# Sparse attention followed by an ELU feed-forward layer: load order, load shapes and the hand-written engine orders rewritten

## The chip, the cores and the metric

The kernel runs on one core of a Trainium2 chip. The metric is device time in microseconds (us), the median of the runs of one build. The core has a matrix engine (TensorE, PE in the profile; its weight loads are PEld), VectorE (DVE), ScalarE (ACT), GpSimd (POOL), SyncE (SP, which here only starts stores and transposing transfers), and 16 DMA engines that move data between memory (HBM) and the on-chip SBUF. PSUM is the accumulator memory; it is used here as two "pairs" of two banks (slots 0 and 1) and four single banks (slots 2 to 5).

## The reference

Inputs are q, k, v of shape (8 batches, 8 heads, 576 positions, 64) in float32. Heads 0 to 3 of each batch use a *local* causal mask (a key counts if it lies 0 to 31 positions back), heads 4 to 7 a *strided* causal mask (a key counts if it lies a multiple of 32 positions back). The attention output is a matrix of 4608 tokens by 512, and it passes through a two-layer network:

```
scores = q @ k.T / 8;  scores = where(mask, scores, -1e9)
attn   = softmax(scores);  x = attn @ v            # x: 4608 tokens x 512
h = x @ w_in                                       # w_in: 512 x 2048
g = where(h > 0, h, exp(min(h, 0)) - 1)            # ELU
out = g @ w_out                                    # w_out: 2048 x 512
```

## The kernel before

All matrix work is in bfloat16; GpSimd's transfers convert from float32 on the way. The work is named by short tokens in one long list, `ORDER` (lines 48 to 147), which the loop at line 797 issues one after the other. Each engine executes its own instructions strictly in that order, so the list decides what each engine queues behind what. A token names its work, `@n` the PSUM slot and `/D`, `/A` or `/S` the engine that copies (DVE, ACT, or a transposing transfer from SP).

Attention tokens begin with batch, kind (`l` local, `s` strided) and head pair (0 or 1). For the first three batches q and k are turned on PE: `tq`, `tk` (lines 434 to 448) transpose into PSUM and `cq`, `ck` (450 to 462) copy back to SBUF. Batches 3 to 7 use `turn`, transposing transfers. `S`, or for batch 0 `s0` and `s1`, computes scores; `e`, `F0`, `F1` (or `e0`, `e1`) are exponentials on ACT; `m0` and `M` multiply by a 0/1 mask on DVE. Where a batch and kind stand in `ADDED` (line 230), the mask is instead added to the scores by extra matmuls with an identity matrix, and no `m` is needed. `v0`, `v1` copy the strided v into place, `halo` copies the last 32 rows of each block of local v in front of the next block (line 496), `a` is probabilities times v, `n` the division by the row sum (a reciprocal and a product on DVE, lines 647 and 649), `x` transposes the result on PE and `y` copies it into `xT`, the input of the network.

The network runs in nine chunks of 512 tokens. In chunk c, `i c.b` (line 725) computes hidden block b of 16 as four matmuls of 128x128 by 512 columns (a third number names one of the four, in the order strided pair 0, strided pair 1, local pair 0, local pair 1); `x` is the exponential (ACT, line 730), `r` the clipping on DVE (line 736) or a ReLU on ACT (line 734), `g` the last step of ELU on DVE (lines 745, 742). `o c.t.p` (line 751) computes quarter p (hidden blocks 4p to 4p+3) of the output of 128 tokens, and `c` copies the finished output to SBUF for its store. `busy.n` are n matmuls on zeros, of no use to the result.

Chunk 0 needs only batch 0; chunk c above 0 needs batches up to c. The loads of the first batches, the masks, the clearing of buffers and the weights are issued by GpSimd in the order of `LOADS` (line 41): `l.q.0` is the local q of batch 0, `s.v.1` the strided v of batch 1, `w.in.2` the third of four quarters of w_in (hidden blocks 8 to 11), `w.out.2` the third quarter of w_out. The strided q and k of batch 0 are issued ahead of the list (line 384). The part of the list from `clear.v.2` on is issued where `load.2` stands in `ORDER`. Later batches are loaded by the tokens `load.3` to `load.7`.

In the kernel before, the strided attention of batch 1 is computed among that of batch 0, ahead of the first matmul of the network, and the rest of batch 1 within chunk 0. The strided v of a batch is loaded by one transfer per head of 90 partitions and one of 18 partitions for what is left (lines 262 to 269); the local v by one transfer (line 274); w_out by four transfers whose partitions take one row of 2 KB from each of four blocks of 128 rows (line 327).

Of the kernel before, what the change touches and what calls it, by code (L numbers as in the profile page):

```python
# [41 lines left out]
l.q.0 s.v.0 l.k.0 s.q.1 mask.cut.0 s.k.1 l.v.0 s.v.1 w.in.0 l.k.1 w.in.1 w.in.2 l.q.1  # L42
w.out.0 w.in.3 clear.str.0 clear.loc.1 clear.loc.2 w.out.1 clear.str.1 w.out.2
clear.loc.0 l.v.1 mask.late.0 w.out.3 clear.v.2 s.q.2 s.k.2 s.v.2 l.q.2 l.k.2 l.v.2
# [4 lines left out]
0s1.tq@2 0s0.tq@3 0s1.cq/D 0s0.cq/D busy.3 0s1.tk@4 0s0.tk@2 0s1.ck/D 0s0.ck/D  # L49
0s0.s0@0 0l0.tq@3 0s0.e0 0l1.tq@4 0l0.cq/A 0s1.s1@1 0l1.cq/D 0s1.s0@0 0s1.e1 0s0.v0/D  # L50
0s0.v1/A 0s0.s1@1 0s1.e0 mk.s 0s0.e1 busy.2 0s1.a@0 0l0.tk@2 0s1.n@0 0l1.tk@3 0l0.ck/A
0s0.a@1 0l1.ck/A 0l0.s0@0 0s0.n@1 load.2 0s1.x@4 1s0.tq@2 0l0.e0 1s1.tq@3 0s1.y/D
0l1.s0@1 1s1.cq/A 0l1.s1@0 1s0.cq/D 0l1.e0 0s0.x@4 1s0.tk@3 0l1.e1 0l0.s1@1 0s0.y/D
1s0.ck/A 1s1.tk@2 0l0.e1 mk.l 1s1.ck/A busy.3 1s0.S@0,1,4,3 0s1.halo/D 1s0.e 1s0.v0/D
1s0.F0 busy.3 0l0.a@0 1s0.v1/D 1s1.e 1s0.m0 0l0.n@0 1s0.F1 busy.1 0l1.a@1 0l1.n@1
busy.2 0l0.x@2 i0.1.0@4 i0.2.0@5 0l0.y/A i0.1.1 i0.0.0@3 1s0.M 0l1.x@0 1s1.m0 i0.0.1
i0.1.2 0l1.y/D i0.0.2 1s0.a@1 i0.0.3 i0.1.3 1s0.n@0 1l0.tk@2 x0.0@0 i0.2.1 x0.1@1
i0.2.2 i0.2.3 r0.0/D 1s0.x@0 r0.1/D 1l1.tk@1 x0.2@2 g0.0 r0.2/D i0.6@3 1l1.ck/D g0.2
1s1.a@1 x0.6@0 g0.1 i0.4@5 1s1.n@1 i0.5@4 x0.4@2 r0.6/D 1s1.x@1 1s0.y/D r0.4/A x0.5@1
g0.4 1s1.y/A 1l1.tq@0 r0.5/D i0.3@5 1l1.cq/A g0.6 g0.5 1l0.tq@1 x0.3@2 i0.7@3 1l0.ck/D  # L60
# [48 lines left out]
o4.1.0@3 5s0.F1 5s1.e 5s0.M c4.0/D o4.1.1 5s1.m0 5s0.a@0 o4.1.2 5s0.n@0 5s1.a@1 o4.1.3
5s1.n@1 5s0.z o4.2.0@4 c4.1/A 6l0.S@0,1,5,2 5s1.z o4.2.1 6l0.e o4.2.2 6l0.F0 6l0.m0  # L110
6l0.F1 6l1.e o4.2.3 6l0.M o4.3.0@3 6l1.m0 c4.2/A o4.3.1 turn.7l o4.3.2 o4.3.3 5s0.y/A
c4.3/D 6s0.v0/D 6s0.S@0,1,5,2 5s1.y/A 6s0.v1/D i5.0@4 6s0.e turn.7s i5.1@3 6s0.F0
6s0.m0 x5.0@1 i5.2@5 6s0.F1 r5.0/D x5.1@2 6s0.M 6s1.e g5.0 i5.3@2 r5.1/D x5.2@0
6s0.a@0 6s1.m0 x5.3@1 g5.1 i5.4@4 r5.2/A r5.3/D x5.4@2 g5.2 i5.5@3 g5.3 r5.4/A i5.6@5
x5.5@0 g5.4 i5.7@2 r5.5/A 6s0.n@0 x5.6@1 o5.0.0@4 x5.7@2 g5.5 6s0.z r5.6/A r5.7/D
i5.8@3 g5.6 6s1.halo/A g5.7 6s1.a@1 i5.9@5 x5.8@0 6s1.n@1 r5.8/A 6l0.a@0 x5.9@1
i5.10@2 g5.8 6s1.z r5.9/A 6l0.n@0 6l1.a@1 x5.10@2 i5.11@3 g5.9 r5.10/A o5.0.1 6l0.y/S
x5.11@0 6l1.n@1 i5.12@5 r5.11/A g5.10 6l1.y/S g5.11 x5.12@1 i5.13@2 r5.12/D i5.14@3
g5.12 6s0.y/A o5.0.2 x5.13@2 x5.14@0 r5.13/D i5.15@5 g5.13 r5.14/A g5.14 o5.1.0@2
x5.15@1 r5.15/D 6s1.y/A o5.1.1 g5.15 o5.1.2 7l0.S@0,1,3,5 o5.0.3 7l0.F1 7l0.F0 7l0.e  # L120
o5.1.3 7l0.M c5.0/D 7l1.e i6.0@5 7l0.m0 c5.1/D i6.1@3 x6.0@2 7l1.m0 i6.2@4 r6.0/D
x6.1@0 g6.0 i6.3@2 r6.1/A x6.2@1 g6.1 i6.4@5 x6.3@2 r6.2/D o5.2.0@3 g6.2 r6.3/A x6.4@0
g6.3 i6.5@4 r6.4/D i6.6@2 g6.4 x6.5@1 7s0.v0/D i6.7@5 r6.5/D x6.6@2 g6.5 o5.2.1 x6.7@0
r6.6/D 7s0.v1/D i6.8@4 g6.6 r6.7/A g6.7 i6.9@2 x6.8@1 i6.10@5 r6.8/D x6.9@2 g6.8
o5.2.2 r6.9/A x6.10@0 g6.9 i6.11@4 r6.10/D o5.2.3 g6.10 x6.11@1 7s0.S@0,1,2,5 r6.11/D
c5.2/A g6.11 i6.12@3 7s0.F1 7s0.F0 7s0.e 7s0.M o5.3.0@4 7s1.e 7s0.m0 i6.13@5
7s1.halo/D x6.12@2 7s0.a@0 7s1.m0 x6.13@0 7l0.a@1 7s0.n@0 o5.3.1 r6.12/A r6.13/A
# [23 lines left out]
def kernel(  # L151
# [75 lines left out]

    E_STR, E_LOC = 3, 3

    ADDED = ('0l', '0s')  # L230
    src = {"q": q, "k": k, "v": v}


# [150 lines left out]
    for name in "qk":  # L384
        load_strided(0, name)
# [603 lines left out]
```

## Time and profile before

| | |
|---|---|
| median of 3 runs | 315.29 us (315.17 to 315.65) |
| the profiled execution | 314.54 us, of which the traced span is 312.7 us |
| PE, PEld busy | 297.9 us (95%), 147.8 us (47%) |
| DVE, ACT busy | 217.5 us (70%), 189.5 us (61%) |
| POOL busy | 136.0 us (43%) |
| granted PE clock | 0.996 of full speed |
| first matmul of the network | 25.16 us after the span's start |

The span runs from the first to the last instruction. An engine's busy time counts each moment once; the "mean ns" of a PE row is the time from issue to the modelled end of one matmul, and since matmuls follow each other in a pipeline, the distance between their starts is what a matmul costs. The chain of work that ended last gives these distances. Its shares: PE 82%, DVE 5%, POOL 4%, DMA 3%.

### The profile page before, as it was taken

What the parts mean: (1) busy time and instruction counts of PE and PEld (TensorE: products, weight loads), DVE (VectorE), ACT (ScalarE), POOL (GpSimd) and SP (SyncE); (2) the same over time, 40 slices, a digit from 0 to 9 for tenths busy, and PEclk for the clock granted to TensorE, in tenths of its full rate; (3) what the DMA queues carried; (4) which work ended last, traced back from release to release, by engine and by line L of the source; (5) the groups of instructions that cost most, each with busy time, mean ns of one, the idle gap of its engine ahead of it and who ended that gap; (6) DMA issues with size and microseconds to landing.
All of it is one profiled execution on the core that took longest, in us unless ns stands there. A gap on an engine that the chain in (4) does not pass through costs nothing.

```text
span 312.7 us, 6031 instructions
## 1 busy us (share of the span) xinstructions
PE 297.9 (95%) x2222; PEld 147.8 (47%) x2262; DVE 217.5 (70%) x424; ACT 189.5 (61%) x346; POOL 136.0 (43%) x207
## 2 busy tenths in 40 slices
PE   8888899999999999999999999999999999999992
PEld 3554446445545544445444454544454444444441
DVE  2578987687969886797288865996888178765300
ACT  4683685686847766565476648986675167555210
POOL 8959954698777776984894500000000000000000
PEclk9999999999999999999999999999999999999998
DMA  6999999999999999999999966731005311012012
GB/s 102 176 160 206 207 170 153 166 82 136 165 152 191 162 155 106 147 223 161 204 150 168 157 127 111 148 61 67 0 36 114 72 31 34 8 39 60 34 69 74
DMA packets 116357, 37.37 MB, mean 119 GB/s; under 512 B 97320, under 2 KB 111280, under 8 KB 116320
## 3 DMA queue, kind: packets, MB, share of 16 engines
q0 software_dynamic: 74240, 18.42, 66.4%
q1 hardware_dynamic: 42080, 18.49, 31.6%
q8 instruction: 19, 0.31, 0.4%
q14 instruction: 18, 0.15, 0.2%
HBM read 36.70 MB, written 9.44 MB: 148 GB/s over the span
## 4 chain that ended last, share of the span: by engine, by line
PE 82%; DVE 5%; POOL 4%; DMA 3%; issue 2%; ACT 2%; POOLq 0%; ACTq 0%
PE single L751 39%; PE single L725 37%; DMA w_in_sb<-in_moe_w_in_dram 3%; PE pair L637 3%; DVE g_sb L745 2%; DVE g_sb L736 2%; POOL v_raw L263 2%; PE pair L544 1%; ACT e_sb L730 1%; PE single L544 1%; PE pair L446 1%; DVE x_s L649 1%; PE pair L657 1%; POOL v_loc L274 0%; POOL v_raw L267 0%
## 5 line engine op out<-in xcount | busy, mean ns | idle before, releaser
L725 PE MATMUL single<-xT,w_in_sb 128*128 128x512 bf16 x555 | 135.7, 379 | 2.9 <-DVE g_sb L745 1.1
L751 PE MATMUL single<-w_out_sb,g_sb 128*128 128x512 bf16 x560 | 134.6, 379 | 1.4 <-issue 0.3
L730 ACT ACTIVATE e_sb<-single 128x512 f32<-128x512 f32 x144 | 85.4, 599 | 71.2 <-PE single L725 67.6
L725 PEld LDWEIGHTS <-w_in_sb 128*128 128x128 bf16 x576 | 54.6, 98 | 65.0 <-issue 2.4
L751 PEld LDWEIGHTS <-g_sb 128*128 128x128 bf16 x576 | 54.4, 98 | 62.5 <-issue 0.5
L745 DVE TENSOR_TENSOR g_sb<-g_sb,single 128x512 bf16<-128x512 bf16 x92 | 62.4, 684 | 2.1
L736 DVE TENSOR_SCALAR g_sb<-e_sb 128x512 bf16<-128x512 f32 x92 | 44.0, 480 | 28.5 <-ACT e_sb L730 27.8
L742 DVE SCALAR_TENSOR_TENSOR g_sb<-e_sb,g_sb 128x512 bf16<-128x512 f32 x52 | 35.5, 686 | 7.5 <-ACT g_sb L734 7.5
L622 ACT ACTIVATE pr<-pair 128x960 bf16<-128x960 f32 (+4 forms) x36 | 31.7, 900 | 6.0 <-PE pair L544 3.2
L734 ACT ACTIVATE g_sb<-single 128x512 bf16<-128x512 f32 x52 | 30.7, 593 | 0.0
L758 ACT COPY o_sb<-single 128x512 f32<-128x512 f32 x23 | 13.5, 587 | 22.6 <-PE single L751 21.8
L263 POOL DMA_DIRECT2D v_raw<-in_v_dram x32 | 20.0, 640 | 3.8 <-DMA v_loc<-in_v_dram 2.2
L637 PEld LDWEIGHTS <-pr 128*128 128x128 bf16 (+3 forms) x364 | 15.3, 102 | 8.6 <-issue 3.1
L758 DVE COPY o_sb<-single 128x512 f32<-128x512 f32 x12 | 8.2, 687 | 13.7 <-PE single L751 13.7
L286 POOL DMA_DIRECT2D k_loc<-in_k_dram x20 | 15.1, 773 | 5.3 <-DMA v_loc<-in_v_dram 2.3
L286 POOL DMA_DIRECT2D q_loc<-in_q_dram x20 | 15.4, 780 | 2.8 <-DMA k_str<-in_k_dram 2.6
L649 DVE TENSOR_TENSOR x_l<-pair,rden 96x768 bf16<-96x768 f32 x16 | 15.3, 954 | 0.6
L649 DVE TENSOR_TENSOR x_s<-pair,rden 126x640 bf16<-126x640 f32 (+1 forms) x16 | 14.0, 874 | 0.5
L626 DVE TENSOR_TENSOR pr<-pr,mask_l 128x960 bf16<-128x960 bf16 x14 | 9.2, 654 | 6.1 <-ACT pr L622 6.1
L263 POOL DMA_DIRECT2D q_str<-in_q_dram x20 | 12.8, 646 | 0.1
L263 POOL DMA_DIRECT2D k_str<-in_k_dram x20 | 12.4, 631 | 1.2 <-DMA q_str<-in_q_dram 0.6
L274 POOL DMA_DIRECT2D v_loc<-in_v_dram x8 | 9.8, 1220 | 2.7 <-issue 1.6
(121 smaller groups left out, 232.7 us busy)
## 6 DMA issues: line engine op xcount, KB each, us to landing
out_dram<-o_sb SPq DMA_DIRECT2D x30, 256.0 KB, 2.8
v_loc<-in_v_dram POOLq DMA_DIRECT2D x8, 288.0 KB, 9.0
v_raw<-in_v_dram POOLq DMA_DIRECT2D x32, 67.5 KB, 6.1
w_in_sb<-in_moe_w_in_dram POOLq DMA_DIRECT2D x4, 512.0 KB, 10.3
w_out_sb<-in_moe_w_out_dram POOLq DMA_DIRECT2D x4, 512.0 KB, 11.6
out_dram<-o_sb SPq DMA_DIRECT2D x12, 128.0 KB, 2.3
q_str<-in_q_dram POOLq DMA_DIRECT2D x20, 67.5 KB, 6.7
k_str<-in_k_dram POOLq DMA_DIRECT2D x20, 67.5 KB, 5.4
```

The source lines that it names most:

```text
L263: nc.gpsimd.dma_start(out=t[0:n, h, 0:run].rearrange("p g d -> p (g d)"), in_=rows[h, :, 0:30, :].rearrange("t (a g) d -> a t (g d)", g=run))
L286: nc.gpsimd.dma_start(out=t[:, h // 2, 0:4, h % 2], in_=src[name][b, h, 0:512].rearrange("(i p) d -> p i d", p=128))
L622: nc.scalar.activation(t, sc[0:t.shape[0], :, 0:w], ACT.Exp, scale=scale)
L637: nc.tensor.matmul(av[0:m, p, blk, :], lhsT=self.pr[0:k, o:o + m], rhs=vt[0:k, 2 * self.hp + p, blk, :], start=True, stop=True)
L649: nc.vector.tensor_tensor(self.x[0:nq, 0:n].rearrange("q g p d -> q p g d"), av[0:nq, :, 0:n, 0:D], rd[0:nq, :, 0:n].unsqueeze(3).to_broad ...
L725: nc.tensor.matmul(h_of[c, i], lhsT=w_in_sb[:, cc, i * 128:(i + 1) * 128], rhs=xT[:, cc, c * N_TILE:(c + 1) * N_TILE], start=j == 0, stop= ...
L730: nc.scalar.activation(e_sb[slot], h_of[c, i], ACT.Exp)
L734: nc.scalar.activation(g[:, i, :], h_of[c, i], ACT.Relu)
L736: nc.vector.tensor_scalar(g[:, i, :], e, scalar1=1.0, scalar2=1.0, op0=ALU.min, op1=ALU.subtract)
L742: nc.vector.scalar_tensor_tensor(g[:, i, :], e, 1.0, g[:, i, :], op0=ALU.subtract, op1=ALU.min)
L745: nc.vector.tensor_tensor(g[:, i, :], g[:, i, :], h_of[c, i], op=ALU.max)
L751: nc.tensor.matmul(out_of[c, i], lhsT=g[:, m, i * 128:(i + 1) * 128], rhs=w_out_sb[:, m, :], start=(m == 0), stop=(m == MC - 1))
```

## The change

`LOADS` has a new order: the weights come ahead of all of batch 1, and the local q and k of batch 0 come ahead of its v. The local q of batch 0 is issued before the identity matrix and the masks are built. The strided v of the first three batches is loaded in six transfers of 18 partitions, each over all four heads; the local v of batch 0 in two transfers, one per pair of heads, and its halo copy is made per pair. w_out is loaded with four consecutive rows on one partition, and so hidden unit p*4+j takes the place that unit j*128+p had; the columns of w_in are therefore read with a step of four when they are loaded as matmul weights (`w_in_part`). Batch 1's local scores get their mask by added matmuls. The mask of the first local block is that of the others. `ORDER` is written anew throughout; the part shown ends where chunk 1 begins.

```diff
 LOADS = """
-l.q.0 s.v.0 l.k.0 s.q.1 mask.cut.0 s.k.1 l.v.0 s.v.1 w.in.0 l.k.1 w.in.1 w.in.2 l.q.1
-w.out.0 w.in.3 clear.str.0 clear.loc.1 clear.loc.2 w.out.1 clear.str.1 w.out.2
-clear.loc.0 l.v.1 mask.late.0 w.out.3 clear.v.2 s.q.2 s.k.2 s.v.2 l.q.2 l.k.2 l.v.2
+l.q.0 l.k.0 s.v.0 mask.cut.0 l.v.0 w.in.0 w.in.1 w.out.0 w.in.2 clear.loc.2 w.in.3
+w.out.1 w.out.2 clear.loc.1 clear.str.1 clear.str.0 l.q.1 l.k.1 s.q.1 mask.late.0
+clear.loc.0 w.out.3 s.k.1 l.v.1 s.v.1 clear.v.2 l.q.2 l.k.2 s.q.2 s.k.2 s.v.2 l.v.2
 ORDER = """
+0s0.tq@2 0s1.tq@3 0s0.cq/D 0s1.cq/D busy.3 0s1.tk@4 0s0.tk@2 0s1.ck/D 0s0.ck/D
+0s0.s0@0 0l0.tq@3 0s0.e0 0s0.s1@1 0l0.cq/A 0l1.tq@4 0s0.e1 0s1.s0@0 0l1.cq/D 0l1.tk@2
+0s1.e0 0l0.tk@3 0l1.ck/A 0s1.s1@1 0l0.ck/D 0l1.s0@0 0s1.e1 0s0.v1/D 0s0.v0/D 0l1.e0
+mk.s busy.1 0l0.s1@1 load.2 0l1.s1@0 0l0.e1 0l1.e1 busy.1 0s0.a@1 0s1.a@0 0s0.n@0
+0l0.halo/A 0s1.n@1 busy.2 0l0.s0@1 0s0.x@4 0l0.e0 busy.1 0s1.x@2 0s0.y/D 0l1.halo/A
+0l0.a@0 mk.l 0s1.y/A 0l1.a@1 0l0.n@0 0l1.n@1 busy.2 0l0.x@3 i0.0.0@4 0l0.y/A i0.1.0@2
+0l1.x@0 i0.2.0@3 i0.0.1 0l1.y/D i0.0.2 i0.0.3 i0.1.1 i0.2.1 x0.0@0 i0.2.2 i0.1.2
+i0.1.3 r0.0/D i0.2.3 i0.3@5 g0.0 x0.1@1 x0.2@2 r0.1/D i0.4@4 g0.1 r0.2/A x0.3@0 g0.2
...
+i0.14@3 g0.12 o0.0.1 r0.15/D
+x0.14@0 g0.15 1l0.tq@5 r0.14/A 1l1.tq@2 g0.14 1l0.cq/A o0.0.2 1l1.cq/A 1l0.tk@5
+1l1.tk@3 1l0.ck/A o0.1.0@2 1l1.ck/A 1s0.tq@5 1s1.tq@3 o0.1.1 1s0.cq/D 1s1.cq/D
+1l0.S@0,1,5,3 o0.0.3 1l0.e o0.1.2 1l0.F0 c0.0/D 1l0.F1 1l1.e 1s0.tk@5 1s1.tk@3 o0.1.3
+1s0.ck/D 1s1.ck/D 1s0.S@0,1,4,5 c0.1/A o0.2.0@3 1s0.e 1s1.halo/D o0.2.1 1s0.F0 1s0.m0
+1s0.F1 1s1.e 1l0.a@0 1s0.M o0.2.2 1s0.v0/D 1s0.v1/D 1s1.m0 1s0.a@1 1l0.n@0 o0.2.3
+o0.3.0@2 1s0.n@0 c0.2/A 1s1.a@0 1s0.x@4 1s1.n@1 1l0.x@5 1l1.a@1 1s0.y/A 2l0.tq@3
+1l0.y/D 1s1.x@4 2l0.cq/A 2l1.tq@0 1l1.n@1 o0.3.1 1s1.y/A 2l1.cq/D 1l1.x@5 2l0.tk@3
+1l1.y/D load.3 2l1.tk@4 2l0.ck/A i1.0@5 2l1.ck/A i1.1@3 x1.0@1 2s0.tq@4 r1.0/D
...
+def w_in_part(w_in_sb, c, i):
+    return w_in_sb[i // 4][:, c].rearrange("k (p j) -> k j p", j=4)[:, i % 4]
-    w_in_sb = consts.tile([128, KC, d_ff], BF16, tag="w_in_sb")
+    w_in_sb = several(consts, 4, "w_in", KC, 512)
-    ADDED = ('0l', '0s')
+    ADDED = ('0l', '0s', '1l')
...
+        if b < E_STR:
+            for a in range(6):
+                r = slice(run * a, min(run * a + run, STRIDE))
+                nc.gpsimd.dma_start(
+                    out=t[NT * a:NT * a + NT, :, 0:r.stop - r.start, :].rearrange(
+                        "p h g d -> p h (g d)"),
+                    in_=rows[:, :, r, :].rearrange("h t g d -> t h (g d)"))
+            return
...
-            nc.gpsimd.dma_start(
-                out=v_loc[b % 3].rearrange("p h i d -> p (h i) d")[32:128, :, 0:D],
-                in_=v[b, 0:4].rearrange("h (i p) d -> p (h i) d", p=LB))
+            for h in (slice(0, 2), slice(2, 4)) if b == 0 else (slice(0, 4),):
+                nc.gpsimd.dma_start(
+                    out=v_loc[b % 3][:, h].rearrange("p h i d -> p (h i) d")[32:128, :, 0:D],
+                    in_=v[b, h].rearrange("h (i p) d -> p (h i) d", p=LB))
...
-            nc.gpsimd.dma_start(out=w_in_sb[:, :, 512 * i:512 * (i + 1)],
+            nc.gpsimd.dma_start(out=w_in_sb[i],
                                 in_=wi[:, :, 512 * i:512 * (i + 1)])
-            nc.gpsimd.dma_start(out=w_out_sb[:, 4 * i:4 * (i + 1), :],
-                                in_=wo[:, 4 * i:4 * (i + 1), :])
+            nc.gpsimd.dma_start(
+                out=w_out_sb[:, 4 * i:4 * (i + 1), :].rearrange("p j d -> p (j d)"),
+                in_=moe_w_out[512 * i:512 * (i + 1)].rearrange("(p j) d -> p (j d)", j=4))
...
     for name in "qk":
         load_strided(0, name)
+    load(LOADS[0])
...
         def halo(self, copy, slot):
             t = v_loc[self.b % 3]
+            if self.b == 0:
+                t = t[:, 2 * self.hp:2 * self.hp + 2]
             copy(t[0:32, :, 1:6, 0:D], t[96:128, :, 0:5, 0:D])
...
-                nc.tensor.matmul(h_of[c, i], lhsT=w_in_sb[:, cc, i * 128:(i + 1) * 128],
+                nc.tensor.matmul(h_of[c, i], lhsT=w_in_part(w_in_sb, cc, i),
```

Counted over the whole list, 82 of the 144 `r` steps are on DVE and 62 on ACT (before 92 and 52), and of the first 35 `c` copies 4 are on DVE and 31 on ACT (before 12 and 23; the last is shared by both in either kernel). The `busy` matmuls in the list are 10 (before 14).

197 lines of the change are left out of this document (89 added, 108 removed).

## The prediction

> **What bounds the kernel now.** I read the page first, then the busy time by stretches, then the chain and single rows of the time order around the first network matmul. The page:
>
> ```profile
> span 312.7 us, 6031 instructions
> ...
> L725 PE MATMUL single<-xT,w_in_sb 128*128 128x512 bf16 x555 | 135.7, 379 | 2.9 <-DVE g_sb L745 1.1
> ...
> L730 ACT ACTIVATE e_sb<-single 128x512 f32<-128x512 f32 x144 | 85.4, 599 | 71.2 <-PE single L725 67.6
> L725 PEld LDWEIGHTS <-w_in_sb 128*128 128x128 bf16 x576 | 54.6, 98 | 65.0 <-issue 2.4
> ...
> L745 DVE TENSOR_TENSOR g_sb<-g_sb,single 128x512 bf16<-128x512 bf16 x92 | 62.4, 684 | 2.1
> L736 DVE TENSOR_SCALAR g_sb<-e_sb 128x512 bf16<-128x512 f32 x92 | 44.0, 480 | 28.5 <-ACT e_sb L730 27.8
> ...
> L734 ACT ACTIVATE g_sb<-single 128x512 bf16<-128x512 f32 x52 | 30.7, 593 | 0.0
> L758 ACT COPY o_sb<-single 128x512 f32<-128x512 f32 x23 | 13.5, 587 | 22.6 <-PE single L751 21.8
> ```
>
> The reader sees that ACT waited 67.6 us for PE, and PE little for anything: PE sets the pace. The stretches tell where it does not (columns: stretch, length, busy us of PE, PEld, DVE, ACT, POOL; at the end clock, DMA share and GB/s):
>
> ```profile
> 10.00:20.00 10.00, 9.11 (x179) 6.21 (x180) 6.01 (x16) 8.46 (x15) 6.05 (x9) 1.00 1.76 161
> 20.00:30.00 10.00, 8.39 (x121) 4.92 (x121) 7.48 (x18) 5.22 (x10) 9.86 (x13) 1.00 1.26 204
> 30.00:40.00 10.00, 8.15 (x69) 4.13 (x71) 9.93 (x19) 6.11 (x12) 9.65 (x15) 1.00 1.25 206
> 40.00:60.00 20.00, 19.84 (x179) 10.48 (x180) 14.02 (x28) 13.21 (x25) 12.04 (x17) 1.00 1.61 165
> 60.00:80.00 20.00, 19.36 (x188) 9.89 (x190) 16.86 (x33) 16.00 (x31) 16.89 (x25) 1.00 1.28 114
> 80.00:300.00 220.00, 217.53 (x1406) 105.20 (x1433) 159.45 (x304) 134.99 (x242) 72.87 (x108) 1.00 0.90 109
> ```
>
> From 40 us on PE idles little: 0.64 us from 60 to 80, 2.47 us from 80 to 300. Ahead of 40 us it idles, and part of its busy time is matmuls on zeros. In 30 to 40 us DVE is busy 9.93 of 10: there batch 1's attention and chunk 0 share it. So the ends to work on are the first network matmul, and DVE right behind it. What released that matmul stands in the order of time and in the chain:
>
> ```profile
> 10.22 0.65 ACT L622 ACTIVATE pr<-pair 108x576 bf16<-108x576 f32 x1 [0.27 <-PE pair L544]
> ```
> ```profile
> 24.30 0.95 DVE L649 TENSOR_TENSOR x_l<-pair,rden 96x768 bf16<-96x768 f32 x1
> ```
> ```profile
> 25.16 1.04 PE L725 MATMUL single<-xT,w_in_sb 128*128 128x512 bf16 x4 [0.54 <-DMA w_in_sb<-in_moe_w_in_dram]
> ```
> ```profile
> 14.93 10.19 DMA w_in_sb<-in_moe_w_in_dram
> ...
> 36.94 0.38 PE pair L446 x12
> ...
> 43.47 2.59 PE single L725 x12
> ...
> 47.94 0.21 PE pair L544 x10
> ...
> 51.96 0.76 PE pair L637 x24
> 52.72 0.52 PE single L440 x16
> ...
> 54.11 0.26 PE single L657 x6
> ```
>
> Two things end together at 25.2 us: the first weights land (14.93 + 10.19 = 25.12) and the last division of batch 0 (24.30 + 0.95 = 25.25). Taking away one alone gives nothing. The chain also prices PE work by start distance: a network matmul is 2.59 / 12 = 0.216, a block or output quarter of four 0.864.
>
> **Term 1, the loads.**
>
> ```profile
> w_in_sb<-in_moe_w_in_dram POOLq DMA_DIRECT2D x4, 512.0 KB, 10.3
> w_out_sb<-in_moe_w_out_dram POOLq DMA_DIRECT2D x4, 512.0 KB, 11.6
> ...
> k_loc<-in_k_dram POOLq DMA_DIRECT2D x3, 288.0 KB, 7.7
> ```
> ```profile
> w_out_sb<-in_moe_w_out_dram POOLq DMA_DIRECT2D x1, 512.0 KB, 10.7
> ```
> ```profile
> 38.48 0.77 POOL L327 DMA_DIRECT2D w_out_sb<-in_moe_w_out_dram  x1
> ```
> ```profile
> POOL w_in_sb L324 <- DMA v_loc<-in_v_dram: 2.5, 1, 2.5
> ```
>
> A load of q, k or v is 288 KB, a quarter of weights 512 KB. Ahead of the first quarter stood nine 288 KB loads; the change leaves six. Three of them are 885 kB; at the 161 to 206 GB/s of the stretches that is 4.3 to 5.5 us, so w.in.0 lands near 20.2. At 205 GB/s a quarter takes 2.56 us and a 288 KB load 1.44: w.in.1 22.8, w.out.0 25.3, w.in.2 27.9, w.in.3 30.5, then w.out.1, w.out.2, l.q.1 37, l.k.1 38.5, s.q.1 40, w.out.3 42.5, s.k.1 44, and s.v.1 near 49, as the last load of the same set did before (38.48 + 10.7). In the program each GpSimd transfer waits for the eighth before it; a 2.5 us wait of that kind is the row above. In the new order what stands in the queue behind each such wait is masks, memsets and further loads, and several 512 KB quarters are always under way, so I cost these waits, the sixth v slice and the split local v at nothing; without that cover a late load costs PE its lateness (first rival).
>
> **Term 2, batch 0's attention.**
>
> ```profile
> L649 DVE TENSOR_TENSOR x_l<-pair,rden 96x768 bf16<-96x768 f32 x16 | 15.3, 954 | 0.6
> ...
> L649 DVE TENSOR_TENSOR x_s<-pair,rden 108x768 bf16<-108x768 f32 x6 | 5.7, 958 | 0.2
> L647 DVE RECIPROCAL rden<-pair 96x12 f32<-96x12 f32 x16 | 3.6, 222 | 1.1 <-PE pair L637 1.1
> ...
> L461 DVE COPY kT_loc<-pair 128x576 bf16<-128x576 bf16 x2 | 1.5, 738 | 0.0
> L686 DVE COPY xT<-single 128x540 bf16<-128x540 bf16 x2 | 1.4, 721 | 0.8 <-PE single L657 0.8
> ...
> L454 DVE COPY kT_str<-single 128x576 bf16<-128x576 bf16 x3 | 1.3, 450 | 0.3 <-PE single L440 0.3
> ```
> ```profile
> L622 ACT ACTIVATE pr<-pair 108x972 bf16<-108x972 f32 x4 | 3.9, 969 | 0.6 <-PE single L544 0.6
> ...
> L461 ACT COPY qT_loc<-pair 128x576 bf16<-128x576 bf16 x4 | 2.6, 640 | 0.1
> ...
> L622 ACT ACTIVATE pr<-pair 128x576 bf16<-128x576 f32 x4 | 2.5, 655 | 0.5 <-PE pair L544 0.5
> ```
>
> The first exponential stays at 10.22: what it needs is not moved. ACT then does seven exponentials of 0.65 and two copies of 0.64, 5.8 us, and with two short waits for PE ends near 16.5. The first division follows at 16.6, and DVE is then the chain: two strided divisions (0.96 plus two reciprocals, 1.2), one copy into xT (0.72 and its small rest, 0.9), the mask (0.3), two local divisions (1.18): 6.0, so 22.6 instead of 25.25. The v loads land by 13 (strided) and 17 (local) and are due at 15.5 and 17 to 19. Batch 0's halo copies now stand on ACT and wait there for the halves of local v; behind them queue the last local exponential, due at 18.5, and the copies into xT, so a half that lands after 18.5 delays the divisions by as much. Weights, at 20.2, no longer decide. The first complete block has all four inputs at 23.7.
>
> **Term 3, chunk 0 and batch 1.** From there DVE spends per block 0.684 and, in about half of them, 0.48: 0.92, against PE's 0.864. PE needs for 16 blocks and two output quarters 15.6 us from 21.9, plus about 1.2 of waits for DVE at start: 38.7. Then 12 quarters (10.4), and attention: local transposes of batches 1 and 2, 8 x 0.38; strided ones of batch 1, 2 x 0.52; scores of 1 1.3; four `a` 1.5, four `x` 1.0: 7.9; the mask of 1l as matmuls, four of 480 and two of 192 columns at 0.216 per 512, 1.0. That is 19.3, plus 1.5 for waits: chunk 1 starts at 59.5. The removed mask products free DVE of about 1.7, which has room here, so I give no gain for that.
>
> ```profile
> 38.75:56.77 18.02, 9.02 (x38) 3.70 (x40) 1.00 1.47 167
> ```
>
> Before, chunk 1 starts at 56.78 (last matmul of the row's stretch; the row is for line 751: 40 weight loads) with 64 + 40 = 104 network matmuls done, after with 64 + 56 = 120. The 16 more are 3.5 us; two batch 2 transposes are local rather than strided, 0.5. The same state before is 56.8 + 3.5 + 0.5 = 60.8. Gain 1.3.
>
> **Term 4, chunks 1 to 8.** In chunk 1 the new order puts batch 2's whole attention between the blocks. ACT: 15 x 0.599, 9 x 0.593, two exponentials of 0.969 and some 3.6 of smaller exponentials and copies (an estimate, seven at about 0.5), 19.9; PE: 16 blocks and two quarters 15.6, attention 3.0, 18.6. ACT exceeds PE by 1.3, against 0.64 of idle PE before: loss 0.5 (ends 0 and 1.3). In the rest, ten `r` and eight `c` move from DVE to ACT: DVE loses some 10 us, ACT gains 10 x 0.593 + 8 x 0.587 = 10.6 of the 85 it has idle from 80 to 300. Only DVE's waits can gain: of 2.47 idle PE I take 0.7 back (ends -1.3, as in chunk 1, and 2.5).
>
> **Term 5, weights read with a step of four.** 1152 - 576 = 576 loads of w_in, 98 ns each now, hidden behind 216 ns. No row shows a strided weight load. The nearest, a DVE copy written with a step of six against one in runs, 738 to 450, is a ratio of 1.64: 161 ns, still hidden, cost 0. The far end is four times 98, 392, of which 176 would show: 101 us. I take 0, since the near row leaves a quarter of the cover.
> By the Trainium skill's page "SBUF — State Buffer" (Door 1: The DMA port swizzle), reads keep full bandwidth while two of them fall on one 16-byte line; a step of four bfloat16 is 8 bytes, so two do, and the sum would be the same by it. No run so far shows it.
>
> Sum: 314.54 - 1.3 + 0.5 - 0.7 = 313.0 for a profiled execution. That one lies 0.75 below the median of the runs, 315.29, so the median after is 313.8.
>
> **The rivals.**
> - *Batch 1 lands too late* (slower). Its loads now queue behind eight quarters. PE needs s.k.1 at 47 in term 3; it lands at 44 at 205 GB/s. Speaking for it: 40 to 60 us ran at 165 GB/s, 10 to 20 at 161, where local v was loaded. From w.in.0 at 20.2 to s.k.1 are 4.85 MB: at 165 GB/s 29.4 us, landing 49.6, a stall of 2.6. It decides from 1.5 us on, or 172 GB/s. Against: 20 to 40 us, the same kinds of loads, ran at 204 to 206. Median 316.4.
> - *ACT becomes the bound in later chunks too* (slower): the excess of chunk 1, 1.3, met in three of the six further attention stretches: -1.3 + 1.3 + 3.9, 319.2; met once, 316.6. Against: from 80 to 300 us ACT is busy 135 of 220, and all that is added is 10.6.
> - *Weights read with a step are not hidden* (slower): from 216 ns on; 300 ns would be 576 x 84 = 48 us, 362.
> - *PE's waits go almost wholly* (faster): with DVE relieved, the 0.64 and 2.47 idle go as well: 315.29 - 1.3 - 3.1 = 310.9.
> - *The lead is eaten*: the waits set at 2.7 in term 3 are 4, and the rest as before: 315.3.
>
> **How the numbers follow.** This kernel's measurement tells 0.2%, 0.63 us, from no change. Forecast 0.45 (own range 312.6 to 314.6), waits gone 0.13, lead eaten 0.13, late loads 0.14, ACT bound 0.12, weights 0.03. Faster is the first two, 0.58; same 0.13; slower 0.29. The range goes from the faster rival to the slower ones without the weights: 310.9 to 316.6.
>
> **What would show it.** First network matmul near 22, last division of batch 0 near 22.6, w.in.0 landed near 20; chunk 1 starting near 59.5 with 120 matmuls done; PE idle in 60 to 80 above 0.64; w_in weight loads at 98 to 161 ns. The prediction is wrong if PE waits on a k, v or w_out transfer between 35 and 55 us, if weight loads pass 216 ns, or if ACT rather than PE releases the later `g` steps.

## The result, and the profile after

The changed kernel takes 321.02 us (median of 6 runs, 319.69 to 326.02) against 315.79 us for the kernel before in the same session (6 runs, 315.17 to 317.06): a ratio of 1.0153, 95% interval 1.0113 to 1.0193. Ratios, here and below, are worked out over the fast runs of both kernels alone (here without the one of 326.02) and can differ by up to 1% from the quotient of the medians. It is slower by 1.5%, where 313.8 us was forecast and the range ended at 316.6. The profiled execution took 319.71 us, 5.17 more than the profiled 314.54 of before; both lie below their medians, so the two traces may be set against each other.

The page of the changed kernel (line 725 is now 739, 751 is 765, 730 is 744, 736 is 750, 745 is 759, 665 is 679, 686 and 688 are 700 and 702):

```profile
span 317.9 us, 6085 instructions
...
L739 PE MATMUL single<-xT,w_in 128*128 128x512 bf16 x576 | 139.2, 382 | 5.6 <-ACT xT L702 3.0
L765 PE MATMUL single<-w_out_sb,g_sb 128*128 128x512 bf16 x576 | 138.8, 379 | 0.2 <-DVE g_sb L759 0.2
L744 ACT ACTIVATE e_sb<-single 128x512 f32<-128x512 f32 x144 | 86.1, 603 | 57.8 <-PE single L739 55.7
L739 PEld LDWEIGHTS <-w_in 128*128 128x128 bf16 x576 | 64.4, 114 | 66.0 <-issue 11.0
```

Ahead of the hidden-block matmuls PE now waits 3.0 us for line 702, a copy into `xT`. Before, the largest such item was 1.1 us for DVE's `g`. ACT still waits 55.7 us for PE, so ACT is not the bound, and a weight load of w_in grew from 98 to 114 ns. The stretches of the changed kernel (same columns as before: PE, PEld, DVE, ACT, POOL, then clock, DMA share, GB/s):

```profile
10.00:20.00 10.00, 9.49 (x172) 6.06 (x173) 5.79 (x16) 7.68 (x13) 9.28 (x15) 1.00 1.41 170
20.00:30.00 10.00, 8.70 (x53) 4.21 (x50) 8.21 (x15) 6.04 (x13) 9.75 (x11) 1.00 1.16 210
30.00:40.00 10.00, 8.94 (x41) 4.31 (x39) 9.14 (x16) 6.61 (x13) 6.67 (x11) 1.00 1.16 210
40.00:60.00 20.00, 19.91 (x305) 12.20 (x302) 11.78 (x26) 10.68 (x22) 11.82 (x20) 1.00 1.57 166
60.00:80.00 20.00, 19.45 (x172) 10.83 (x167) 16.82 (x36) 17.64 (x34) 18.43 (x28) 1.00 1.28 108
80.00:300.00 220.00, 215.91 (x1431) 110.02 (x1430) 153.46 (x291) 141.90 (x256) 72.52 (x109) 0.99 0.90 107
...
154.00:156.00 2.00, 0.14 (x1) 0.11 (x1) 0.00 (x0) 1.48 (x3) 1.11 (x2) 1.00 1.34 242
156.00:158.00 2.00, 1.18 (x4) 0.40 (x3) 0.00 (x0) 1.49 (x3) 1.94 (x5) 0.70 1.32 213
158.00:160.00 2.00, 2.00 (x7) 0.63 (x6) 0.67 (x2) 0.60 (x1) 2.00 (x3) 0.50 1.03 169
160.00:162.00 2.00, 2.00 (x10) 1.05 (x9) 1.03 (x2) 1.58 (x3) 2.00 (x4) 0.95 1.45 140
```

Up to 80 us this is close to the forecast. From 80 to 300 us PE idles 4.09 us instead of 2.47, and 2.68 of it lie in two of the last rows: from 154 to 158 us PE is mostly idle, and from 156.8 to 160.2 us the granted clock is a half. The order of time there, in the changed kernel (start, length, engine, what; idle time and releaser in brackets):

```profile
152.66 1.03 PE L765 MATMUL single<-w_out_sb,g_sb 128*128 128x512 bf16 x4
...
154.52 1.16 ACT L700 COPY xT<-qT_str 128x540 bf16<-128x540 bf16 x1 [3.67 <-DMA qT_str<-x_s]
...
155.86 0.38 PE L739 MATMUL single<-xT,w_in 128*128 128x512 bf16 x1 [2.18 <-ACT xT L702]
...
157.06 5.15 PE L739 MATMUL single<-xT,w_in 128*128 128x512 bf16 x16 [0.82 <-ACT xT L702]
```

This is the first block of chunk 4. It needs the strided output of batch 4, which from batch 4 on does not go through PE: SP's transposing transfer (the token `z`, line 679) turns it, and ACT copies the result into `xT` (`y`, lines 700 and 702). ACT waited 3.67 us for that transfer and PE 2.18 + 0.82 for the two copies. In the kernel before the same place looks like this:

```profile
145.12 1.20 SPq L665 DMA_TRANSPOSE qT_str<-x_s  x1
...
154.96 0.23 ACT L688 COPY xT<-qT_str 128x36 bf16<-128x36 bf16 x1
...
155.80 2.75 PE L725 MATMUL single<-xT,w_in_sb 128*128 128x512 bf16 x12
```

The second copy ended at 155.19 and PE arrived at 155.80, 0.6 us later. But this copy had not waited for its transfer: issued at 145.12, the transfer had landed at 150.96, and the copy stood behind ACT's copy of an output (c3.1), which waited for PE. In the changed kernel 1.35 us pass from the landing to the end of the copies (155.65 to 157.00); by that, the data could have been in place at 152.3, 3.5 us ahead of PE. The new order puts eight instead of eleven output quarters of chunk 3 ahead of chunk 4, so PE arrives at 153.7, and its `z` are issued later. Why later is in the queue of SP, which issues strictly in order (changed kernel; the waits first, then the order of time):

```profile
SPq L309 <- DMA q_str<-in_q_dram: 9.2, 1, 9.2
```
```profile
118.63 1.00 SPq L780 DMA_DIRECT2D out_dram<-o_sb  x2
129.00 2.13 SPq L309 DMA_TRANSPOSE qT_str<-q_str  x1
132.11 1.55 SPq L309 DMA_TRANSPOSE kT_str<-k_str  x1
...
134.63 3.42 SPq L315 DMA_TRANSPOSE qT_loc<-q_loc  x2
138.13 3.71 SPq L315 DMA_TRANSPOSE kT_loc<-k_loc  x2
141.94 1.23 SPq L685 DMA_TRANSPOSE xT<-x_l  x1
...
145.55 2.79 SPq L679 DMA_TRANSPOSE qT_str<-x_s  x2
```

SP stood 9.2 us for batch 5's strided q (the token `turn.5s`). Batch 5's local transposes (`turn.5l`) queued behind it, and batch 4's outputs behind those. The data of the two `z` were ready at about 141.3 and 143.5 (ends of their divisions); they were issued at 145.55 and 146.89 and landed at 154.44 and 155.65, 8.9 and 8.8 us later, among the loads of batch 6.

The 5.17 us divide as follows: 3.00 of waiting, 1.7 of half clock (2 x 0.30 + 2 x 0.50 + 2 x 0.05 from the three rows above; 0.13 of it falls into the waiting), and some 0.5 left. Up to the last matmul of the network nothing else is lost on balance: it starts at 306.69 before and 311.39 now, 4.70 later. The 0.5 lie behind it, where the span ends 6.50 us after this start instead of 6.04.

### The profile page after: what moved, and what is told of

The parts are those of the page before. It is cut to its first block, busy times and chain, and to the rows that moved or that the text cites. A ratio compares the mean times of both kernels' runs of the same rounds, so it can differ in the third digit from the quotient of the medians.

```text
span 317.9 us, 6085 instructions
## 1 busy us (share of the span) xinstructions
PE 302.8 (95%) x2264; PEld 156.6 (49%) x2264; DVE 209.6 (66%) x407; ACT 196.3 (62%) x361; POOL 136.7 (43%) x210
## 4 chain that ended last, share of the span: by engine, by line
PE 65%; DMA 13%; POOL 8%; DVE 5%; issue 4%; ACT 2%; DVEq 0%; ACTq 0%; POOLq 0%
PE single L765 30%; PE single L739 26%; DMA q_str<-in_q_dram 5%; DMA q_loc<-in_q_dram 3%; DMA qT_str<-x_s 3%; PE pair L651 2%; DMA k_str<-in_k_dram 2%; POOL k_loc L299 2%; PE single L407 2%; PE pair L558 2%; POOL q_loc L299 2%; DVE g_sb L750 1%; DVE g_sb L759 1%; POOL v_loc L287 1%; POOL q_str L275 1%
## 5 line engine op out<-in xcount | busy, mean ns | idle before, releaser
L739 PE MATMUL single<-xT,w_in 128*128 128x512 bf16 x576 | 139.2, 382 | 5.6 <-ACT xT L702 3.0
L765 PE MATMUL single<-w_out_sb,g_sb 128*128 128x512 bf16 x576 | 138.8, 379 | 0.2 <-DVE g_sb L759 0.2
L744 ACT ACTIVATE e_sb<-single 128x512 f32<-128x512 f32 x144 | 86.1, 603 | 57.8 <-PE single L739 55.7
L739 PEld LDWEIGHTS <-w_in 128*128 128x128 bf16 x576 | 64.4, 114 | 66.0 <-issue 11.0
L750 DVE TENSOR_SCALAR g_sb<-e_sb 128x512 bf16<-128x512 f32 x82 | 37.5, 458 | 49.9 <-ACT e_sb L744 49.4
L759 DVE TENSOR_TENSOR g_sb<-g_sb,single 128x512 bf16<-128x512 bf16 x82 | 56.4, 688 | 3.1
L756 DVE SCALAR_TENSOR_TENSOR g_sb<-e_sb,g_sb 128x512 bf16<-128x512 f32 x62 | 42.2, 688 | 3.8 <-ACT g_sb L748 3.4
L772 ACT COPY o_sb<-single 128x512 f32<-128x512 f32 x31 | 18.2, 587 | 30.0 <-PE single L765 29.5
L748 ACT ACTIVATE g_sb<-single 128x512 bf16<-128x512 f32 x62 | 36.6, 599 | 0.0
L269 POOL DMA_DIRECT2D v_raw<-in_v_dram x18 | 10.9, 613 | 4.6 <-DMA w_out_sb<-in_moe_w_out_dram 2.7
L275 POOL DMA_DIRECT2D v_raw<-in_v_dram x20 | 12.2, 626 | 1.3 <-DMA q_str<-in_q_dram 0.9
L640 DVE TENSOR_TENSOR pr<-pr,mask_l 128x960 bf16<-128x960 bf16 x12 | 7.9, 656 | 7.0 <-ACT pr L636 6.9
```

Of the source, the lines that this page charges most:

```text
L275: nc.gpsimd.dma_start(out=t[0:n, h, 0:run].rearrange("p g d -> p (g d)"), in_=rows[h, :, 0:30, :].rearrange("t (a g) d -> a t (g d)", g=run))
L739: nc.tensor.matmul(h_of[c, i], lhsT=w_in_part(w_in_sb, cc, i), rhs=xT[:, cc, c * N_TILE:(c + 1) * N_TILE], start=j == 0, stop=j == KC - 1)
L744: nc.scalar.activation(e_sb[slot], h_of[c, i], ACT.Exp)
L748: nc.scalar.activation(g[:, i, :], h_of[c, i], ACT.Relu)
L750: nc.vector.tensor_scalar(g[:, i, :], e, scalar1=1.0, scalar2=1.0, op0=ALU.min, op1=ALU.subtract)
L756: nc.vector.scalar_tensor_tensor(g[:, i, :], e, 1.0, g[:, i, :], op0=ALU.subtract, op1=ALU.min)
```

## The experiments

Theory A, from the trace: one late wait at chunk 4, made dearer by the clock, cost nearly all of it, and the rest of the change is worth about nothing or a little. Theory B: a loss spread over the kernel, from slower weight loads or a fuller ACT. The first four kernels ran on one chip, where the kernel before took 314.59 us (median, 313.92 to 318.95).

**The local transposes first.** Two tokens change places in `ORDER`.

```diff
-... g3.3 turn.5s o2.1.3 ... load.6 turn.5l 4l0.e ...
+... g3.3 turn.5l o2.1.3 ... load.6 turn.5s 4l0.e ...
```

> Against the changed kernel only the places of turn.5l and turn.5s in ORDER are exchanged, so that SyncE's queue is done with batch 5's local transposes before batch 4's strided output is divided. Theory A (the lost time is one wait: batch 4's strided output, turned by a DMA transpose, is queued behind other transposes on SyncE and then behind loads, PE waits 3.0 us for it and its clock is halved for 3.4 us after): the two transposes start near 141.5 and 143.6 instead of 145.55 and 146.89, PE does not wait at the start of chunk 4, the clock stays at 1.0, and the profiled execution falls by 4 to 5 us from 319.7 to about 315. Theory B (the loss is spread: slower weight loads and a fuller ScalarE; the wait only takes up time that PE would lose anyway): the wait goes but at most 1 us with it, 318.7 or more.

Measured: 314.86 us (314.12 to 315.76), ratio to the kernel before 0.9987 (0.9957 to 1.0017). The profiled execution took 314.43, and its clock never fell. SP and PE in it:

```profile
118.37 3.56 SPq L315 DMA_TRANSPOSE qT_loc<-q_loc  x2
...
142.07 4.17 SPq L679 DMA_TRANSPOSE qT_str<-x_s  x2
...
153.63 7.72 PE L739 MATMUL single<-xT,w_in 128*128 128x512 bf16 x35
```

The local transposes now start as soon as the stores are out, at 118.4 instead of 134.6; the first `z` starts at 142.07; and PE goes into chunk 4 at 153.63 without a wait. One swap of two tokens gives back 5.3 us of the profiled time.

**The loads of batch 6 held back.** GpSimd waits, by a copy of one element out of `xT`, until batch 4's outputs have landed, before it issues batch 6's local v and strided loads; SP's order stays that of the change.

```diff
-... 4s1.y/A o3.1.3 i4.0@4 ...
+... 4s1.y/A hold.6 more.6 o3.1.3 i4.0@4 ...
+        elif what == "hold":
+            nc.gpsimd.tensor_copy(held, xT[0:1, 3, 5 * S - 1:5 * S])
```

> Against the changed kernel GpSimd holds the local v and the strided loads of batch 6 until batch 4's strided output is in xT, so that the two output transposes meet fewer packets; SyncE's order stays as it is. If the other loads make the transpose slow: start still 145.5, landing after about 5 us instead of 8.9, by 151, no PE wait, about 315. If only SyncE's queue counts: landing near 154, PE still waits about 3 us, about 319.7. Theory B: 319 or more in either case.

Measured: 315.71 us (314.92 to 316.59), ratio 1.0015 (0.9981 to 1.0048).

```profile
145.05 2.54 SPq L689 DMA_TRANSPOSE qT_str<-x_s  x2
...
150.97 1.17 ACT L710 COPY xT<-qT_str 128x540 bf16<-128x540 bf16 x1
...
153.74 7.58 PE L749 MATMUL single<-xT,w_in 128*128 128x512 bf16 x34
```

(This kernel is ten lines longer above these places: 679 is 689, 700 is 710, 739 is 749.) The two transfers are issued nearly as late as in the changed kernel (145.05 and 146.37) but land 3.3 and 2.6 us later instead of 8.9 and 8.8. So the late issue alone does no harm; it does when other loads are under way. Either remedy is enough. Both together (below) gave nothing more.

**PE kept busy through the wait.** Fourteen matmuls on zeros, 3.0 us, ahead of chunk 4.

```diff
-... o3.1.3 i4.0@4 ...
+... o3.1.3 busy.14@2 i4.0@4 ...
```

> Against the changed kernel 14 matmuls on zeros (3.0 us) are put where PE waits at the start of chunk 4, so that it does not stand still; their result is not used. Theory A: the late output stays late, but the clock is not halved: 1.7 us better than the changed kernel, profiled near 318.0, clock 1.0 from 156 to 160 us. Theory B: no gain, 319.7.

Measured: 319.89 us (317.90 to 321.96), ratio 1.0145 (1.0101 to 1.0188); the profiled execution took 320.4.

```profile
153.87 3.18 PE L407 MATMUL single<-xT 128*128 128x512 bf16 x14
157.82 0.38 PE L739 MATMUL single<-xT,w_in 128*128 128x512 bf16 x1 [0.77 <-ACT xT L702]
159.02 2.32 PE L739 MATMUL single<-xT,w_in 128*128 128x512 bf16 x10 [0.82 <-ACT xT L702]
```

Here the clock stayed at 1.00 through these stretches: with PE busy it does not fall. But in this execution the first `z` started only at 147.79, and real work began at 159.02, two microseconds later than in the changed kernel. Three of the ten runs lay at 317.9 to 318.0, as expected, the others above. The clock's part is shown in the profile; its price of 1.7 us is not confirmed by the times.

**Weights read in one run.** The old loads of w_out, and w_in's columns contiguous again.

```diff
-    return w_in_sb[i // 4][:, c].rearrange("k (p j) -> k j p", j=4)[:, i % 4]
+    return w_in_sb[i // 4][:, c, 128 * (i % 4):128 * (i % 4) + 128]
```

> Against the changed kernel w_out is loaded as before and the columns of w_in are read in runs of 128 again. Theory A: weight loads of w_in fall from 114 to 98 ns, but both are hidden behind the 216 ns of a matmul: within 0.7 us of the changed kernel, wait at chunk 4 still there, 319 to 320.5. Theory B: 576 loads times 16 ns, up to 9 us better, 311 to 316.

Measured: 321.88 us (318.09 to 326.43), ratio 1.014 (1.0023 to 1.0257).

```profile
L739 PEld LDWEIGHTS <-w_in 128*128 128x128 bf16 x576 | 55.6, 98 | 75.1 <-issue 12.9
```

The load is back at 98 ns, the wait at chunk 4 is still there (3.3 us for line 702), and no gain shows, though with so few runs the interval is wide. With a step of four a load takes 16 ns longer, and no cost of it shows. Theory B falls in this part, and the swap above leaves it nothing else of size.

The next five ran on a chip on which the kernel before took 315.10 us (313.88 to 320.43), except the second of the two with the new start, for which another chip is named.

**The old load order.** On top of the swap, `LOADS` as before the change.

```diff
-l.q.0 l.k.0 s.v.0 mask.cut.0 l.v.0 w.in.0 w.in.1 w.out.0 w.in.2 ...
+l.q.0 s.v.0 l.k.0 s.q.1 mask.cut.0 s.k.1 l.v.0 s.v.1 w.in.0 l.k.1 w.in.1 ...
```

> The changed kernel with the local transposing transfers of batch 5 ahead of the strided ones (as in the run that lost the late wait, 314.9 us), and with the load order of the kernel before (batch 1's strided q, k and v and its local k ahead of or among the weights). Everything else as changed. Theory A (the load order gave a real lead, which the late wait at chunk 4 hid): the first quarter of weights lands at about 25 again instead of 19.5, the first network matmul near 25.2 to 26, and most of those 4 to 5 us are lost again, since batch 1's early data has no early consumer in this order: 317 to 320 us. Rival (the order of the loads is worth nothing here, and what PE does ahead of 60 us is set by DVE's divisions and blocks): 314.5 to 315.5 us.

Measured: 323.46 us (321.18 to 324.23), ratio 1.0226 (1.0169 to 1.0283).

```profile
25.75 0.60 PE L739 MATMUL single<-xT,w_in 128*128 128x512 bf16 x2
...
31.96 0.41 PE L739 MATMUL single<-xT,w_in 128*128 128x512 bf16 x1 [1.83 <-DMA w_in<-in_moe_w_in_dram]
...
38.42 1.04 PE L765 MATMUL single<-w_out_sb,g_sb 128*128 128x512 bf16 x4 [2.82 <-DMA w_out_sb<-in_moe_w_out_dram]
```
```profile
10.00:20.00 10.00, 8.06 (x102) 4.26 (x103) 2.31 (x6) 5.57 (x10) 7.03 (x13) 0.67 1.50 140
...
30.00:40.00 10.00, 5.35 (x25) 2.54 (x25) 7.02 (x11) 4.30 (x9) 9.71 (x16) 1.00 1.19 211
```

The first quarter of weights lands at 25.08 (19.47 in the changed kernel), PE waits for the next ones, and between 30 and 40 us it is busy 5.35 us instead of 8.94. More is lost than expected (323.46 against the 314.86 of the swap): besides the late start PE is starved by the later quarters, and its clock is a half from 13.5 to 20.3 us. So in the new order of work the new load order is worth 7.5 us by the ratios and 8.6 by the medians (of two chips). The new order of work needs the new loads; what the new loads would be worth under the old order of work was not run.

**The new start with the old rest.** From chunk 1 on the order of the kernel before; batch 2's strided q and k turned ahead of chunk 1; o0.3's first quarters done ahead of it.

```diff
-... 2l0.tq@3 ... o0.3.1 ... load.3 2l1.tk@4 2l0.ck/A i1.0@5 2l1.ck/A ...
+... 2s0.tq@3 ... o0.3.1 ... load.3 2s1.tk@2 2s0.ck/A 2s1.ck/D 2s0.v1/D 2s0.v0/A i1.0@2 ...
```

> The new start (loads, batch 0 and 1, chunk 0) joined to the order of the kernel before from chunk 1 on; what differs from both: batch 2's strided q and k are turned ahead of chunk 1 instead of its local ones, and the four quarters o0.2 and o0.3 that the old order had inside chunk 1 are done ahead of it, so that only two quarters are left within it. Theory A (the start gains about 1, and the new order of chunks 1 to 3 gives it back, on top of the late wait): 313.3 to 314.2 us, chunk 1 starting near 60 with 120 network matmuls done, and no wait of PE for the copies into xT at chunk 4. Rival (the start gains nothing that lasts): 314.6 to 315.5 us.

Measured: 317.79 us (316.36 to 320.49), ratio 1.0065 (1.0027 to 1.0104): a miss for both theories. There is no late wait at chunk 4, but between 70 and 80 us PE idles 1.86 us (0.40 before; the 3.0 of the next expectation is too high), most of it for DVE's divisions of batch 2, where the old chunk 1 had quarters of output to fill the gaps of batch 2's attention and this one has only two.

**The same with chunk 1 filled.** o0.3 stays inside chunk 1, o0.2 is finished ahead of it.

```diff
-... o0.2.3 o0.3.0@4 1s0.n@0 ... o0.3.1 ... i1.0@2 ... o0.3.2 ... o0.3.3 ...
+... o0.2.3 1s0.n@0 ... i1.0@2 ... o0.3.0@3 ... o0.3.1 ... o0.3.2 ... o0.3.3 ...
```

> The new start joined to the old order from chunk 1 on, as in the run of 317.8 us, which left only two output quarters inside chunk 1 and lost 3.0 us of PE between 70 and 80 us. Here o0.3's four quarters stay inside chunk 1, where the kernel before has them; o0.2's last two are done ahead of it. Theory A (the start gains 1 or more, and that loss came from the missing quarters): the loss from 70 to 80 falls below 1.5 us and the time comes to 313.6 to 314.8 us. Rival (the old rest does not fit the new start whatever fills chunk 1): 316 us or more.

Measured, on a chip on which the kernel before took 314.52 us (313.19 to 317.94): 316.80 us (316.01 to 319.97), ratio 1.0081 (1.0046 to 1.0116). The idle time from 70 to 80 us fell to 0.55, as theory A has it, and yet the time did not follow. The waits of PE from 40 to 80 us (lines stand three higher here: 558 is 555, 671 is 668, 759 is 756):

```profile
PE single L555 <- DVE g_sb L756: 1.2, 1, 1.2
PE single L668 <- DVE x_l L660: 0.8, 1, 0.8
PE single L668 <- DVE x_s L660: 0.5, 1, 0.5
```

The loss moved: 1.3 us to the transposes of batch 1's output (at 55.4 and 58.1), among which the quarters had stood, and 1.2 to batch 2's scores (at 70.1). Neither run keeps a lead. The likely reading is that the quarters that are "ahead" at chunk 1 are what covers the attention there, and can be spent once.

**Both remedies together.** The swap and the held loads.

> Both remedies for the late wait together: batch 5's local transposing transfers ahead of the strided ones, and batch 6's local v and strided loads held until batch 4's outputs have landed in xT. Each alone gave 314.9 and 315.7. Theory A (one late wait, and either remedy takes it away whole): nothing more to gain, 314.4 to 315.7 us, no wait of PE at chunk 4, transposing transfers of batch 4 issued near 142 and 145 and taking 2.6 to 3.3 us each. Rival (each remedy alone leaves part of the wait): 313 to 314.2 us.

Measured: 315.12 us (314.51 to 318.10), ratio 0.9988 (0.9952 to 1.0025), with no wait at chunk 4: nothing more to gain there, as expected. The expected length of the transfers was a miss. Issued at 142.51 and 144.74, they took 7.0 and 5.2 us, not 2.6 to 3.3: batch 6's local q and k, which are not held, were still landing until 149.79 (until 146.50 in the run with the held loads alone).

**The mask of 1l multiplied in.** The swap, `ADDED` without `'1l'`, and the tokens `1l0.m0`, `1l0.M` and `1l1.m0`.

```diff
-    ADDED = ('0l', '0s', '1l')
+    ADDED = ('0l', '0s')
```

> As the run with batch 5's local transposing transfers first (314.9 us), but the mask of batch 1's local scores multiplied in on DVE again (three products, about 1.7 us) instead of added by extra matmuls on PE (about 1.0 us). If PE's work is what counts in 40 to 60 us: 313.6 to 314.2 us. If DVE has no room there after all: 314.9 to 316 us. No difference beyond 0.3 us if the two cancel.

Measured: 314.61 us (313.58 to 315.64), ratio 0.9972 (0.9942 to 1.0001), the lowest ratio of all kernels here, though its interval still reaches no change. Against the swap alone (0.9987) the difference lies within both intervals: no difference between the two ways of masking is shown.

**One copy moved.** On top of that, ACT's copy of batch 4's strided v goes behind the local exponentials. A first version moved it past the token that loads batch 6's v into the same buffer. It therefore waited for that load, and batch 4's strided pair 1 was computed with batch 6's v.

```diff
-... c2.1/A g3.5 4s0.v1/A 4l0.S ... load.6 ... i3.8@5 4l1.e 4l0.M ...
+... c2.1/A g3.5 4l0.S ... load.6 ... i3.8@5 4l1.e 4s0.v1/A 4l0.M ...
```

> As the run in which batch 1's local mask is multiplied in on DVE (314.6 us against 315.1 for the kernel before), with one more token moved: ACT's copy of batch 4's strided v (0.83 us) goes from ahead of the exponential of block 6 of chunk 3 to behind the local exponentials. There PE waited 0.52 us for an exponential of batch 4 at 129.7. Theory A (in chunks 1 to 3 the new order keeps ACT and DVE so full that a single copy ahead of an exponential is seen by PE): that wait shrinks to at most 0.2 us and the time comes to 314.1 to 314.4 us. Rival (DVE's block steps hold PE at that place as well): the wait stays within 0.1 us of 0.52, under another name, and the time at 314.6.

Measured: 347.12 us (346.11 to 350.39), where the kernel before took 314.76 (313.49 to 316.91). With ACT waiting 30.5 us for that load, it says nothing on the question. The next version moves the loads of batch 6 behind the copy as well (on this chip the kernel before took 314.52 us, 313.19 to 317.94):

```diff
-... i3.8@5 4l1.e 4s0.v1/A 4l0.M ...
+... i3.8@5 4l1.e 4s0.v1/A load.6 4l0.M ...
```

> As the run in which batch 1's local mask is multiplied in on DVE (314.6 us), with ACT's copy of batch 4's strided v (0.83 us) moved from ahead of the exponential of block 6 of chunk 3 to behind the local exponentials, and the loads of batch 6, whose v goes to the buffer that this copy reads, moved behind it. Theory A (a single copy ahead of an exponential is seen by PE in chunks 2 and 3): the wait of 0.52 us at 129.7 shrinks to at most 0.2 us and the time comes to 314.1 to 314.4 us. Rival (DVE's block steps hold PE at that place as well): the wait stays within 0.1 us of 0.52, under another name, and the time at 314.6.

Measured: 314.88 us (314.07 to 318.50), ratio 1.0033 (0.9997 to 1.007). The wait of 0.52 shrank to 0.2, as theory A says, but nothing was won:

```profile
144.23 3.50 SPq L679 DMA_TRANSPOSE qT_str<-x_s  x2
...
154.04 7.28 PE L739 MATMUL single<-xT,w_in 128*128 128x512 bf16 x33 [0.82 <-ACT xT L702]
```

The `z` now start at 144.23, 2.2 us later than in the run with the swap, and land at 151.42 and 152.48; PE waits 0.8 us at chunk 4 again. Seven of the twelve runs lie between 314.07 and 314.99, four between 316.59 and 318.50. Whether the transfer came later still in the upper four is not shown: the kernel before, without this wait, has runs up to 317.94 on the same chip.

## Why the prediction was wrong

**Term 1, the loads: right.** First weights forecast at 20.2, landed at 19.47; the last load of batch 1 forecast near 49, landed at 47.28; s.k.1 forecast at 44, landed at 42.16. PE waits for none of them, so the rival "batch 1 lands too late" did not come.

**Term 2, batch 0's attention: right.** The last division ends at 22.27, forecast 22.6:

```profile
21.32 0.95 DVE L663 TENSOR_TENSOR x_l<-pair,rden 96x768 bf16<-96x768 f32 x1
```
```profile
21.47 0.60 PE L739 MATMUL single<-xT,w_in 128*128 128x512 bf16 x2
```

**Term 3: right in kind, 0.6 short.** Chunk 1 starts at 60.09 with 120 matmuls done instead of 59.5, which by the term's own working is a lead of 0.7 in place of 1.3. That it needs the new loads is shown by the run with the old load order.

**Term 4, chunks 1 to 8: the step that failed, in two places.** The larger: this term went through the chunks by PE, ACT and DVE, and gave no line to SP: it put the wait for batch 4's turned output at nothing, without a reason. Batches from 3 on are turned by SP's transfers, and so are the outputs from batch 4 on; the new order issues `turn.5s`, `turn.5l` and the two `z` later, and leaves fewer quarters to cover them. The prediction neither listed SP's queue nor asked how long before its use the second transfer arrived, a margin of 3.5 us with its copies. In the new order PE arrives 2.1 us earlier (153.7 against 155.80), the transfer is issued 1.8 us later (146.89 against 145.12) and takes 2.9 us longer (8.76 against 5.84): 6.8 us against a margin of 3.5. The price, 3.0 of waiting and 1.7 of clock, is the whole slowdown: without it the ratio is 0.9987 (0.9957 to 1.0017), no clear change, and not the forecast gain either.

The smaller: the term took 0.7 back out of "2.47 idle PE" from 80 to 300 us. Half of that was no idle time. In the trace of before, 23 starts of 512-column matmuls in this stretch lie 0.43 us apart, twice the distance of 0.216, with a matmul record missing between them; they add up to 1.22 of the 2.47. The row of line 725 said so, x555 where the weight loads are x576. The true reserve was 1.25. In the run with the swap, PE idles 1.28 there:

```profile
60.00:80.00 20.00, 19.29 (x164) 10.66 (x163) 17.04 (x35) 17.43 (x34) 18.64 (x29) 1.00 1.28 112
...
70.00:80.00 10.00, 9.41 (x72) 5.05 (x71) 9.83 (x21) 9.39 (x20) 8.64 (x15) 1.00 1.18 129
...
80.00:300.00 220.00, 218.72 (x1452) 111.82 (x1452) 153.99 (x292) 141.89 (x256) 72.22 (x109) 1.00 0.95 109
```

and 0.71 from 60 to 80, against 1.25 and 0.64 before: of the 0.7, nothing came back. Chunk 1 is full on both sides: from 70 to 80 us DVE is busy 9.83 of 10 and ACT 9.39. The lead of term 3 is used up on the way. At chunk 4 both orders have done the same attention, and the new one has 12 matmuls (2.6 us) fewer behind it; PE is there at 153.7, so it is 0.5 behind the 155.80 of before. PE's waits between 60 and 132 us add up to 1.65 in the changed kernel and, without the places of missing records, to 1.05 before, which shows 0.6 of the loss; where the rest went is open. At chunk 6, where both have done the same 736 matmuls of the network, its first matmul starts at 214.66 before and at 214.62 in the run with the swap: apart from the late wait, the change is worth nothing in the end, which in its size is the rival "the lead is eaten", though that one had the whole lead go in chunk 0, and 0.7 of it was still there at chunk 1.

**Term 5, weights with a step of four: right.** 114 ns, between the forecast's 98 and 161, and hidden. The Trainium skill's page "SBUF — State Buffer" (Door 1) would have had no loss of bandwidth: the time agrees with that, the 16 ns more per load do not.

**The rivals.** All that ended slower asked what PE, ACT or the first 60 us might do. The one that happened, a wait on a transposing transfer at 155 us, was not among them, though the rows of SP and of line 688 stood in the trace. The loads of batches 3 to 7 and the `z` stood in the sum at nothing, without a number for how far ahead of their use they arrive. A gain of 1.5 us would also have been harder to tell than the prediction reckoned: the intervals of most runs here reach 0.3 to 0.4% to each side, not 0.2%.

## What to carry to other kernels

When an order is dealt anew, take every queue that issues in order, SP's and GpSimd's too, and for each transfer whose result another engine needs write down how long before its use it arrives; a margin of a few microseconds (3.5 here) is a term of the sum, not cover. Read it from the landing of the transfer, not from the copy behind it, which may be late for another reason. Put a transfer whose input is ready ahead of one that must still wait for its input, since in an in-order queue the second delays all behind it. Before counting idle time as a reserve, hold the count of records against the count that the program issues.

## What the runs showed of the hardware

- The two transposing transfers from SBUF to SBUF took 8.9 and 8.8 us in the changed kernel, 7.0 and 5.8 before, 7.0 and 5.2 with both remedies, and 3.3 and 2.6 with the held loads alone. In the changed kernel they landed in the order of issue among GpSimd's loads: the loads issued at 145.44 and 146.04 landed at 153.53 and 154.80, the transfer issued between them, at 145.55, at 154.44. That order is not strict: before, the first transfer (137.16 to 144.20) overtook the local v, issued at 136.98 and landed at 146.33.
- A gap of 3 us in PE's work, with one matmul in it, was followed by 3.4 us at half clock (156.8 to 160.2), and a like gap in the run with weights read in one run by as much (158.0 to 161.4). Gaps of 0.8 us were not (in the run with the moved copy, and twice in the run with matmuls on zeros), nor was one of 2.8 us without any matmul (35.6 to 38.4 in the run with the old load order): the length of a gap alone does not decide. The Trainium skill's page "TensorE: Matmul & The Clock Gate" (Part 1: The HAM clock gate) has the clock fall after an idle window of about 3.4 us and come back after a busy one of that length. The length of the half-clock stretch agrees with the second; the gap of 3 us was shorter than the first and not wholly empty.
- A weight load with a step of four elements took 114 ns against 98 ns, without any cost that the times show behind matmuls that start every 216 ns.
